# Thresholded attention and a two-layer MLP on one core: the inverses of the softmax sums computed on VectorE alone, a step earlier

## The chip, the cores and the metric

The kernel runs on one core of one Trainium2 chip. The metric is the device time of one execution in microseconds (us); lower is better. The engines go by short names: PE is TensorE (PEld its weight loads), DVE is VectorE, ACT is ScalarE, POOL is GpSimd, SP is SyncE, which issues DMAs. Each engine works through its own queue in order; between engines, semaphores tell when data are ready.

## The reference

q, k and v have 8 batches x 8 heads x 576 rows x 64; the MLP goes from 512 to 2048 and back.

```python
scale = 1.0 / np.sqrt(q.shape[-1])
scores = scale * np.matmul(q, k.transpose(0, 1, 3, 2))
thresh = np.max(scores, axis=-1, keepdims=True) - tau          # tau = 0.02
scores = np.where(scores >= thresh, scores, -1000000000.0)
scores = scores - np.max(scores, axis=-1, keepdims=True)
attn = np.exp(scores)
attn = attn / (np.sum(attn, axis=-1, keepdims=True) + 1e-09)
x = np.matmul(attn, v)                  # heads side by side: 4608 x 512
h = x @ w_in                            # 512 -> 2048
g = np.maximum(0.01 * h, h)
return g @ w_out                        # 2048 -> 512
```

The change concerns one small piece: the row sums of attn, with 1e-9 added, inverted, and brought into the layout in which the product with v is scaled by them.

## The kernel before

**Tiling.** Two heads make a pair, two pairs a couple: 32 pairs, 16 couples. A couple has nine steps (t = 0 to 8); each step computes the scores of 128 rows for two heads, all 576 columns. The main loop runs over c = 0 to 16 and t = 0 to 8; here, block c means the nine steps of couple c. Block 16 has no scores left, only the rest of the work.

**One step.** TensorE computes the scores (`s_mm`, L158) with hi and lo halves in fp16: twelve matmuls into two tiles `s` of two PSUM banks each. VectorE reads each tile, scales it into `sn` and takes the row's extreme into `nmx` (`s_max`, L181), first half (h = 0), then second (h = 1). POOL makes the threshold `nth` out of it (L186). ScalarE takes exp into `e` (L191). One step later VectorE masks (`s_mask`, L214): weights into `W`, and the row sums into one column of `den`, 18 columns for a couple (9 steps x 2 halves). Where `direct` is set, ScalarE does the second half's mask and exp alone (L197 `far`, L201 `W`, with the row sum), and VectorE has one mask less. A transposing DMA on SP's queue brings `W` into `wT` (L220).

**Other work in the steps.** `prep` (steps 6, 7, 8 and 0) turns a new pair's q or k on TensorE into the bank pair `A` (L129); ScalarE makes `hi` of it (L138), and VectorE `lo` (L139). The lo is put off to the end of the step (the list `soon`, behind the masks). `values` (steps 3 and 5) multiplies `wT` with v into `A` (L279); VectorE scales by `rc` into `xT` (L289). The MLP is cut into units, of which each step takes some (`work`): first-layer units (L301, with ScalarE's `gM`, L305) and second-layer units (L316, with ScalarE's `osb`, L327). They share two PSUM banks `u`. A step places half of its units between the two halves of `s_max` and the rest behind. Step 1 takes two or three units from block 3 on; blocks 1 and 2 have none there.

**The sums.** The sums of couple c-1 are complete behind the last mask, `s_mask(c-1, 8)`, which is queued in step 0 of block c. Then, before the change:

- `sums_0`, end of step 0, behind lo: POOL adds 1e-9 (L228, `d1`).
- `sums_1`, step 1, behind VectorE's sn of the first half: VectorE inverts (L234, `rr`), POOL scales by 2048 and rounds to fp16 (L235, `r2[:, 0]`).
- `sums_2`, step 1, behind sn of the second half: VectorE subtracts, which leaves the rounding's remainder in fp16 (L240, `r2[:, 1]`).
- `sums_3`, step 1, ahead of the step's last unit: TensorE turns `r2` with one matmul against the identity (L246) into a bank pair `A`, and ScalarE copies it to `row` (L249).
- `sums_4`, steps 2 and 4: TensorE spreads `row` over the heads with `sel` (L263), ScalarE copies into `rc` (L268), which `values` needs in steps 3 and 5.

There is a single bank pair `A`: prep, sums_3, sums_4 and values follow one another in it, each when its reader is done. The order of the instructions is written out by hand (a manual schedule); each engine keeps it.

Of the kernel before, what the change touches and what calls it, by code (L numbers as in the profile page):

```python
# [11 lines left out]
OP = mybir.AluOpType  # L12
# [4 lines left out]
def kernel(  # L17
# [10 lines left out]
    nc = tc.nc  # L28
# [10 lines left out]
    RS = 1.0 / 2048.0  # L39
# [9 lines left out]
    r2 = sb.tile([128, 2, 64], FP16, name="r2")  # L49
# [61 lines left out]
    soon = []  # L111

    def take(fs):
        r = list(fs)
        fs.clear()
        return r

    def run(fs):
        for f in fs:
            f()  # L120
# [44 lines left out]
    live, dens = {}, {}  # L165

    def s_max(c, t, h, direct):


        s_ = sc[(c, t)][h]  # L170
        if t == 0 and h == 0:
            dens[c] = sb.tile([128, 18], FP32, tag="den", bufs=2, name="den")
        if h == 0:
            sn = sb.tile([128, 2, 576], FP32, tag="sn", bufs=3, name="sn")
            nmx = sb.tile([128, 2], FP32, tag="nmx", bufs=4, name="nmx")
            nth = sb.tile([128, 2], FP32, tag="nth", bufs=4, name="nth")
            e = sb.tile([128, 2, 576], FP16, tag="e", bufs=3, name="e")
            live[(c, t)] = (sn, nmx, nth, e, Ws[wn[0] % len(Ws)], set())
            wn[0] += 1
        sn, nmx, nth, e, w, masked = live[(c, t)]  # L180
        nc.vector.tensor_scalar(  # L181
            out=sn[:, h, :].rearrange("p (a b) -> p a b", a=2), in0=s_[:, :, 0:288],
            scalar1=-BS, scalar2=None, op0=OP.mult, op1=OP.min,
            accum_out=nmx[:, h:h + 1],
        )
        nc.gpsimd.tensor_scalar(  # L186
            out=nth[:, h:h + 1], in0=nmx[:, h:h + 1], scalar1=1.0, scalar2=tau_f,
            op0=OP.mult, op1=OP.add,
        )
        if not direct:  # L190
            nc.scalar.activation(  # L191
                out=e[:, h, :], in_=sn[:, h, :], func=AF.Exp, bias=nmx[:, h:h + 1], scale=-1.0,
            )
        else:
            masked.add(h)
            far = sb.tile([128, 576], FP32, tag="far", bufs=2, name="far")
            nc.scalar.activation(  # L197
                out=far[:, :], in_=sn[:, h, :], func=AF.Prelu, bias=nth[:, h:h + 1], scale=-1.0,
                alpha=BIG,
            )  # L200
            nc.scalar.activation(  # L201
                out=w[:, ds(h * 576, 576)], in_=far[:, :], func=AF.Exp, bias=ntau[:, 0:1], scale=1.0,
                accum_out=dens[c][:, 2 * t + h:2 * t + h + 1],
            )
# [14 lines left out]
        q0 = 512 if t == 8 else t * 128 + (t // 4) * 128  # L219
        nc.sync.dma_start_transpose(out=wTs[c][:, :, ds(q0, 128)], in_=w[:, :])  # L220

    inv, rows, rcs = {}, {}, {}

    def sums_0(c):

        d1 = sb.tile([128, 18], FP32, tag="d1", bufs=1, name="d1")
        rr = sb.tile([128, 18], FP32, tag="rr", bufs=1, name="rr")
        nc.gpsimd.tensor_scalar(out=d1[:, :], in0=dens.pop(c)[:, :], scalar1=1.0, scalar2=1e-9,  # L228
                                op0=OP.mult, op1=OP.add)
        inv[c] = (d1, rr)  # L230

    def sums_1(c):
        d1, rr = inv[c]
        nc.vector.reciprocal(out=rr[:, :], in_=d1[:, :])  # L234
        nc.gpsimd.tensor_scalar(out=r2[:, 0, 0:18], in0=rr[:, :], scalar1=1.0 / RS, scalar2=0.0,  # L235
                                op0=OP.mult, op1=OP.add)

    def sums_2(c):
        d1, rr = inv[c]
        nc.vector.scalar_tensor_tensor(out=r2[:, 1, 0:18], in0=rr[:, :], scalar=1.0 / RS, in1=r2[:, 0, 0:18],  # L240
                                       op0=OP.mult, op1=OP.subtract)

# [132 lines left out]
    def work(n):  # L375
        for _ in range(min(n, len(units))):
            units.pop(0)[1]()

    with tc.manual_schedule():
        nc.scalar.preload_act_table_set("natural_log_exp_and_others")  # L380
        for i, tail in ((0, 0), (1, 0), (0, 1), (1, 1)):
            load_qk(0, i, tail)
        make_identity(nc, I32)
        nc.vector.tensor_copy(out=I16[:, :], in_=I32[:, :])
        nc.vector.memset(ntau[:, :], -tau_f)
        nc.vector.memset(r2[:, :, :], 0.0)
        nc.vector.tensor_tensor(
            out=sel[:, :, :], in0=I32[:, 0:18].unsqueeze(2).to_broadcast([128, 18, 64]),
            in1=I32[:, 64:82].unsqueeze(2).to_broadcast([128, 18, 64]), op=OP.add,
        )  # L390
        nc.vector.tensor_scalar(out=sel[:, :, :], in0=sel[:, :, :], scalar1=RS, scalar2=None, op0=OP.mult)
        for t in Vs:
            nc.vector.memset(t[64:128, :, 0, 4, :], 0.0)
            nc.vector.memset(t[0:64, :, 1, 0, :], 0.0)
        for p in range(1, 3):
            for i in range(2):
                for tail in range(2):
                    load_qk(p, i, tail)
        prep(0, 0)
        prep(0, 1, "s", 2)  # L400
        run(take(soon))
        share = (23, 27, 23, 13, 23, 13, 23, 23, 23)
        credit = 0.0
        w_at = [1 + i for i in range(32)]
        prev = None
        for c in range(NC + 1):
            last = c == NC
            for t in range(NT):
                step = c * NT + t
                if c > 1 and c % 2 == 0 and t == 6:  # L410

                    if c % 4 == 2 and c > 2:
                        push_tail(c // 2 - 3, 1)
                    push_main(c // 2 - 1)
                    if c % 4 == 0:
                        push_tail(c // 2 - 2, 0)
                    if last:
                        push_tail(c // 2 - 2, 1)
                if not last:
                    s_mm(c, t)  # L420


                nxt = {6: (2 * c + 2, 0), 7: (2 * c + 2, 1), 8: (2 * c + 3, 0), 0: (2 * c + 1, 1)}
                if c == 0:
                    nxt[0], nxt[1] = (1, 0), (1, 1)
                pi = nxt.get(t)
                if pi is not None and pi[0] >= NP:
                    pi = None
                if c == 0 and t < 2:
                    prep(*pi)  # L430
                    pi = None

                if c > 0 and t in (3, 5):
                    values(c - 1, t // 2 - 1)

                ahead = [share[i % NT] for i in range(step, (c // 2 * 2 + (0 if c % 2 == 0 and t < 6 else 2)) * NT + 6)]
                credit = min(credit, 1.0) + (len(units) - credit) * share[t] / sum(ahead)
                n = min(int(credit + 0.01), len(units))
                credit -= n
                if not last:  # L440


                    direct = tau_f <= 16.0 and (
                        t not in (3, 7) if c < 3 else t in (3, 5) or not any(u[0] for u in units[:n]))
                    s_max(c, t, 0, False)
                if c > 0 and t == 1:
                    sums_1(c - 1)
                work(n - n // 2)
                if pi is not None:
                    prep(*pi)  # L450
                if c > 0 and t in (2, 4):
                    sums_4(c - 1, t // 2 - 1)
                if not last:
                    s_max(c, t, 1, direct)
                if c > 0 and t == 1:
                    sums_2(c - 1)
                    work(n // 2 - 1)
                    sums_3(c - 1)
                    work(1 if n > 1 else 0)
                else:  # L460
                    work(n // 2)
                if prev is not None:
                    s_mask(*prev)
                    prev = None
                if not last:
                    prev = (c, t)
                run(take(soon))
                if c > 0 and t == 0:
                    sums_0(c - 1)
                if c == 0 and 0 < t < 6:  # L470
                    load_v(0, t - 1)
                if c % 2 == 0 and c > 0 and t >= 4 and c // 2 < B:
                    load_v(c // 2, t - 4)
                for i in range(32):
                    if w_at[i] == step:
                        load_w(i)
                if t < 4 and 2 * c + 3 < NP:
                    load_qk(2 * c + 3, t // 2, t % 2)
                elif 4 <= t < 8 and 2 * c + 4 < NP:
                    load_qk(2 * c + 4, t // 2 - 2, t % 2)  # L480
        work(len(units))
# [35 lines left out]
```

## Time and profile before

| | us |
|---|---|
| median of 3 runs | 540.46 (540.03 to 541.8) |
| span of the profiled execution | 538.3 |
| blocks 5 to 8 (152 to 274 us) | 122.0, PE busy 119.4, ACT 106.8, DVE 105.6, POOL 42.4 |

The span goes from the first to the last instruction of one profiled execution; a run's time also has what lies around it. Three groups of instructions as the page gives them (line, engine, operation, tiles, shape, count; busy us, mean ns; idle before, and what ended it):

```
L181 DVE TENSOR_SCALAR_CACHE_REDUCE sn<-s 128x576 f32<-128x576 f32 x288 | 206.5, 750 | 49.3 <-PE s L158 49.1
L191 ACT ACTIVATE e<-sn,nmx 128x576 f16<-128x576 f32 x196 | 150.5, 769 | 32.4 <-DVE sn L181 32.2
L214 DVE SCALAR_TENSOR_TENSOR W<-sn,nth,e 128x576 f16<-128x576 f32 x196 | 155.6, 814 | 0.0
```

An instruction with an accumulator output is followed by a short row, DVE_READ_ACCUMULATOR, which writes the accumulated column. In a timeline, a row has its start and length in us, the engine, line, operation and tiles, and in brackets how long the engine was idle before it and who ended that. Neighbouring rows of VectorE overlap in the record: the next one starts before the end of the one in front.

### The profile page before, as it was taken

To read this page: it belongs to the slowest core of one execution; us is meant where nothing else is said; L and a number is where in the kernel's file an instruction comes from. 1 tells how busy PE (TensorE), PEld (TensorE's weight loads), DVE (VectorE), ACT (ScalarE), POOL (GpSimd) and SP (SyncE) were. 2 spreads that over 40 slices of the span, in tenths; PEclk is the share of its full clock that TensorE was granted. 3 is DMA by queue.
4 is the path that set the end of the run, shared out by engine and by line. 5 is a ranking of instruction groups with operands and counts; after the bars stand their busy time and mean duration, and the time that the engine had idled before them with its cause. 6 is when DMAs were issued, how large, how long until landed. Compare 5 with 4: busy or idle time off the path is not lost.

```text
span 538.3 us, 12333 instructions
## 1 busy us (share of the span) xinstructions
PE 497.8 (92%) x4384; PEld 272.8 (51%) x4384; DVE 421.7 (78%) x1106; ACT 433.8 (81%) x765; POOL 188.1 (35%) x430
## 2 busy tenths in 40 slices
PE   5678679899999999999999999999999999999996
PEld 3345454454545565454545566455545566445444
DVE  4897989988899878987899878987899878982000
ACT  3887879899878989889888989889888989884622
POOL 0754556443433334222432234323432234331000
PEclk9676969999999999999999999999999999999999
DMA  6999999998998699778999799777998699654001
GB/s 151 150 202 161 175 182 214 200 180 173 172 165 136 139 169 196 140 137 153 183 155 143 132 182 185 142 135 159 183 155 136 132 187 135 111 89 106 39 40 58
DMA packets 266814, 80.50 MB, mean 150 GB/s; under 512 B 251905, under 2 KB 264193, under 8 KB 266753
## 3 DMA queue, kind: packets, MB, share of 16 engines
q1 hardware_dynamic: 249136, 70.68, 72.3%
q0 software_dynamic: 17536, 8.92, 14.2%
q8 instruction: 34, 0.56, 0.4%
q14 instruction: 28, 0.22, 0.1%
q10 hardware_dynamic: 80, 0.13, 0.1%
HBM read 36.70 MB, written 9.44 MB: 86 GB/s over the span
## 4 chain that ended last, share of the span: by engine, by line
PE 43%; ACT 25%; DVE 16%; issue 8%; DMA 4%; POOL 3%; SPq 0%; DVEq 0%; ACTq 0%; POOLq 0%
PE u L316 13%; DVE sn L181 11%; PE u L301 10%; PE s L158 10%; PE A L279 8%; ACT e L191 7%; ACT far L197 5%; ACT W L201 5%; DVE W L214 3%; ACT gM L305 3%; ACT hi L138 3%; POOL nth L186 3%; DMA nat<-in_q_dram 2%; DVE lo L139 1%; ACT rc L268 1%
## 5 line engine op out<-in xcount | busy, mean ns | idle before, releaser
L181 DVE TENSOR_SCALAR_CACHE_REDUCE sn<-s 128x576 f32<-128x576 f32 x288 | 206.5, 750 | 49.3 <-PE s L158 49.1
L186 POOL TENSOR_SCALAR nth<-nmx 128x1 f32<-128x1 f32 x288 | 127.4, 442 | 251.7 <-DVE sn L181 229.5
L191 ACT ACTIVATE e<-sn,nmx 128x576 f16<-128x576 f32 x196 | 150.5, 769 | 32.4 <-DVE sn L181 32.2
L214 DVE SCALAR_TENSOR_TENSOR W<-sn,nth,e 128x576 f16<-128x576 f32 x196 | 155.6, 814 | 0.0
L301 PE MATMUL u<-xT,win 128*128 128x512 f16 x512 | 128.9, 380 | 2.5 <-ACT gM L305 2.5
L316 PE MATMUL u<-wout,gM 128*128 128x512 f16 x512 | 126.2, 380 | 0.0
L158 PEld LDWEIGHTS <-hi 64*128 64x128 f16 (+1 forms) x1280 | 65.1, 99 | 70.2 <-issue 54.9
L158 PE MATMUL s<-hi,hi 64*128 64x288 f16 x512 | 86.2, 300 | 10.3 <-DVE sn L181 8.8
L158 PE MATMUL s<-lo,hi 64*128 64x288 f16 (+1 forms) x640 | 92.2, 294 | 0.0
L158 PE MATMUL s<-hi,lo 64*128 64x288 f16 (+1 forms) x640 | 92.1, 294 | 0.0
L301 PEld LDWEIGHTS <-win 128*128 128x128 f16 x768 | 58.7, 98 | 56.5 <-issue 20.1
L305 ACT ACTIVATE gM<-u 128x512 f16<-128x512 f32 x128 | 74.6, 588 | 11.7 <-PE u L301 11.7
L197 ACT ACTIVATE far<-sn,nth 128x576 f32<-128x576 f32 x92 | 71.0, 771 | 13.8 <-POOL nth L186 11.6
L201 ACT ACTIVATE W<-far,ntau 128x576 f16<-128x576 f32 x92 | 71.3, 775 | 3.0
L316 PEld LDWEIGHTS <-gM 128*128 128x128 f16 x512 | 44.7, 98 | 51.3 <-issue 12.3
L139 DVE SCALAR_TENSOR_TENSOR lo<-A,hi 128x512 f16<-128x512 f32 (+1 forms) x63 | 47.6, 756 | 14.2 <-ACT hi L138 13.7
L129 PE MATMUL A<-I,nat 128*128 128x128 f32 x283 | 44.6, 288 | 9.9 <-DVE lo L139 4.7
L279 PE MATMUL A<-wT,V 128*64 128x288 f16 x640 | 47.5, 297 | 1.5 <-ACT rc L268 1.1
L129 PEld LDWEIGHTS A<-I,nat 128*128 128x128 f32 x283 | 35.2, 147 | 25.2 <-DVE lo L139 10.0
L138 ACT ACTIVATE hi<-A 128x512 f16<-128x512 f32 (+1 forms) x63 | 40.0, 636 | 7.6 <-PE A L129 7.6
L279 PEld LDWEIGHTS <-V 128*64 128x64 f16 x640 | 36.6, 113 | 11.9 <-issue 8.4
L158 PEld LDWEIGHTS <-lo 64*128 64x128 f16 (+1 forms) x640 | 32.1, 99 | 12.6 <-issue 8.9
(44 smaller groups left out, 292.1 us busy)
## 6 DMA issues: line engine op xcount, KB each, us to landing
nat<-in_q_dram SPq DMA_DIRECT2D x32, 256.0 KB, 3.8
nat<-in_k_dram SPq DMA_DIRECT2D x32, 256.0 KB, 3.9
out_dram<-osb SPq DMA_DIRECT2D x16, 512.0 KB, 3.0
wT<-W SPq DMA_TRANSPOSE x144, 3.9
V<-in_v_dram POOLq DMA_DIRECT2D x8, 256.0 KB, 6.1
win<-in_moe_w_in_dram POOLq DMA_DIRECT2D x16, 128.0 KB, 5.2
V<-in_v_dram POOLq DMA_DIRECT2D x16, 128.0 KB, 4.7
wout<-in_moe_w_out_dram POOLq DMA_DIRECT2D x16, 128.0 KB, 4.3
```

What stands on the lines that cost most here:

```text
L129: nc.tensor.matmul(out=pt[0:128, ds(c * 128, 128)], lhsT=t[0:128, 4 * i + c, :, :].rearrange("p h d -> p (h d)"), rhs=I32[:, :], is_transp ...
L158: nc.tensor.matmul(out=out[h][po, half, 0:288], lhsT=qk[p][i][a][r, cols], rhs=qk[p][1][b][r, ds(half * 288, 288)], start=(ti == 0), stop= ...
L181: nc.vector.tensor_scalar(out=sn[:, h, :].rearrange("p (a b) -> p a b", a=2), in0=s_[:, :, 0:288], scalar1=-BS, scalar2=None, op0=OP.mult, ...
L186: nc.gpsimd.tensor_scalar(out=nth[:, h:h + 1], in0=nmx[:, h:h + 1], scalar1=1.0, scalar2=tau_f, op0=OP.mult, op1=OP.add,)
L191: nc.scalar.activation(out=e[:, h, :], in_=sn[:, h, :], func=AF.Exp, bias=nmx[:, h:h + 1], scale=-1.0,)
L197: nc.scalar.activation(out=far[:, :], in_=sn[:, h, :], func=AF.Prelu, bias=nth[:, h:h + 1], scale=-1.0, alpha=BIG,)
L201: nc.scalar.activation(out=w[:, ds(h * 576, 576)], in_=far[:, :], func=AF.Exp, bias=ntau[:, 0:1], scale=1.0, accum_out=dens[c][:, 2 * t + ...
L214: nc.vector.scalar_tensor_tensor(out=w[:, ds(h * 576, 576)], in0=sn[:, h, :], scalar=nth[:, h:h + 1], in1=e[:, h, :], op0=OP.is_le, op1=OP ...
L279: nc.tensor.matmul(out=t[ds(h * 64, 64), half, 0:288], lhsT=vb[:, g, h, kb, :], rhs=wT[:, 4 * h + kb, ds(e * 576 + half * 288, 288)], star ...
L301: nc.tensor.matmul(out=t[:, ts(j, N)], lhsT=w_in16[:, gi, ts(j0 + j, 128)], rhs=xs[gi], start=(gi == 0), stop=(gi == NG - 1), skip_group_c ...
L305: nc.scalar.activation(out=g_out, in_=t[:, 0:nj * N].rearrange("p (j n) -> p j n", j=nj), func=AF.Prelu, bias=0.0, scale=1.0, alpha=0.01)
L316: nc.tensor.matmul(out=t[:, :], lhsT=g_in(j), rhs=w_out16[:, j, :], start=(j == 0), stop=(j == NJ - 1), skip_group_check=True,)
```

## The change

Add, reciprocal, multiply and subtract all go to VectorE and stand in one function, `sums_0`, which is queued in step 0 directly behind the last mask (and its transposing DMA), ahead of the put-off `lo`. POOL has no part in it any more; `sums_1` and `sums_2` are gone. `sums_3` (the turn on TensorE and ScalarE's copy) stays in step 1 and moves up: it stands behind the first half of the step's units and ahead of sn of the second half. The rest of the units then follow in one piece.

```diff
     def sums_0(c):
         d1 = sb.tile([128, 18], FP32, tag="d1", bufs=1, name="d1")
         rr = sb.tile([128, 18], FP32, tag="rr", bufs=1, name="rr")
-        nc.gpsimd.tensor_scalar(out=d1[:, :], in0=dens.pop(c)[:, :], scalar1=1.0, scalar2=1e-9,
-                                op0=OP.mult, op1=OP.add)
-        inv[c] = (d1, rr)
-
-    def sums_1(c):
-        d1, rr = inv[c]
+        nc.vector.tensor_scalar(out=d1[:, :], in0=dens.pop(c)[:, :], scalar1=1e-9, scalar2=None, op0=OP.add)
         nc.vector.reciprocal(out=rr[:, :], in_=d1[:, :])
-        nc.gpsimd.tensor_scalar(out=r2[:, 0, 0:18], in0=rr[:, :], scalar1=1.0 / RS, scalar2=0.0,
-                                op0=OP.mult, op1=OP.add)
-
-    def sums_2(c):
-        d1, rr = inv[c]
+        nc.vector.tensor_scalar(out=r2[:, 0, 0:18], in0=rr[:, :], scalar1=1.0 / RS, scalar2=None, op0=OP.mult)
         nc.vector.scalar_tensor_tensor(out=r2[:, 1, 0:18], in0=rr[:, :], scalar=1.0 / RS, in1=r2[:, 0, 0:18],
                                        op0=OP.mult, op1=OP.subtract)
...
                     s_max(c, t, 0, False)
+                work(n - n // 2)
                 if c > 0 and t == 1:
-                    sums_1(c - 1)
-                work(n - n // 2)
+                    sums_3(c - 1)
                 if pi is not None:
                     prep(*pi)
...
                 if not last:
                     s_max(c, t, 1, direct)
-                if c > 0 and t == 1:
-                    sums_2(c - 1)
-                    work(n // 2 - 1)
-                    sums_3(c - 1)
-                    work(1 if n > 1 else 0)
-                else:
-                    work(n // 2)
+                work(n // 2)
                 if prev is not None:
                     s_mask(*prev)
                     prev = None
                 if not last:
                     prev = (c, t)
-                run(take(soon))
                 if c > 0 and t == 0:
                     sums_0(c - 1)
+                run(take(soon))
```

More of the change, by code (lines that the diff above doesn't have):

```diff
@@ L220, in s_mask @@
         nc.sync.dma_start_transpose(out=wTs[c][:, :, ds(q0, 128)], in_=w[:, :])
-    inv, rows, rcs = {}, {}, {}
+    rows, rcs = {}, {}
     def sums_0(c):
```

## The prediction

> **What bounds the kernel now.** I read the page's busy shares, then the list of waits, then the timeline around the steps that the change touches.
>
> ```profile
> PE 497.8 (92%) x4384; PEld 272.8 (51%) x4384; DVE 421.7 (78%) x1106; ACT 433.8 (81%) x765; POOL 188.1 (35%) x430
> ```
>
> No engine fills the span, so each stage has to be read by itself. The steps are chained: the scores of a step (TensorE, L158) wait until VectorE has read both halves of the step before (L181), and L181 waits for the scores. A delay of one is a delay of all that follows.
>
> ```profile
> PEld L246 <- DVE r L240: 17.4, 16, 2.6
> PE A L246 <- DVE r L240: 9.1, 12, 2.1
> ```
>
> The list of waits (us in total, times, longest): the little turn of the inverted sums (L246) holds TensorE's in-order queue. The matmul's own idle time is 9.1 us, and that is all the change can take from TensorE; the weight load's 17.4 lies mostly under running matmuls. By the timelines at blocks 1 to 15 (block c is the nine steps of couple c; the turned sums are those of couple c-1) the idle times are 2.11, 1.55, 1.33, 0.86, 0.34, 0.10, 0.40, 0.61, 0.34, 0.10, 0.40, 0.44, 0.34, 0.10, 0.40; 0.07 in block 16.
>
> ```profile
> 277.35 0.09 DVE L214 DVE_READ_ACCUMULATOR W<-sn,nth,e 128x1 f32 x1
> 277.35 0.82 DVE L139 SCALAR_TENSOR_TENSOR lo<-A,hi 128x640 f16<-128x640 f32 x1
> ...
> 278.09 0.75 DVE L181 TENSOR_SCALAR_CACHE_REDUCE sn<-s 128x576 f32<-128x576 f32 x1
> ...
> 278.76 0.27 DVE L234 RECIPROCAL rr<-d 128x18 f32<-128x18 f32 x1
> ...
> 278.94 0.70 DVE L181 TENSOR_SCALAR_CACHE_REDUCE sn<-s 128x576 f32<-128x576 f32 x1
> 278.94 0.78 ACT L191 ACTIVATE e<-sn,nmx 128x576 f16<-128x576 f32 x1 [0.57 <-DVE sn L181]
> ...
> 279.56 0.18 DVE L240 SCALAR_TENSOR_TENSOR r<-rr,r 128x18 f16<-128x18 f32 x1
> 279.62 1.06 ACT L305 ACTIVATE gM<-u 128x512 f16<-128x512 f32 x2
> 279.64 0.82 DVE L214 SCALAR_TENSOR_TENSOR W<-sn,nth,e 128x576 f16<-128x576 f32 x1
> ...
> 279.79 0.23 PE L246 MATMUL A<-I,r 128*128 128x128 f16 x1 [0.34 <-DVE r L240]
> ...
> 280.25 1.02 PE L301 MATMUL u<-xT,win 128*128 128x512 f16 x4 [0.23 <-ACT gM L305]
> ...
> 281.21 0.30 PE L158 MATMUL s<-hi,hi 64*128 64x288 f16 x2
> ```
>
> Block 9, steps 0 and 1 (start, length, idle before). VectorE goes without a pause from the mask to lo, to sn of step 1: here VectorE sets the time. ScalarE's exp (L191) idles 0.57 us for that sn; behind it stand the gM copies; the unit behind L246 waits for the first gM (0.23), since there are two u banks; the scores of step 2 follow at 281.21. So the chain from VectorE's step 0 to the scores of step 2 has no slack, and it does not go through L246.
>
> ```profile
> 306.97 0.08 DVE L214 DVE_READ_ACCUMULATOR W<-sn,nth,e 128x1 f32 x1
> ...
> 307.55 0.82 DVE L139 SCALAR_TENSOR_TENSOR lo<-A,hi 128x640 f16<-128x640 f32 x1 [0.50 <-ACT hi L138]
> ...
> 309.99 0.23 PE L246 MATMUL A<-I,r 128*128 128x128 f16 x1
> 310.06 1.03 PE L316 MATMUL u<-wout,gM 128*128 128x512 f16 x4
> ...
> 311.02 0.30 PE L158 MATMUL s<-hi,hi 64*128 64x288 f16 x2
> ```
>
> Block 10, where the units are of the second layer (L316). One mask on VectorE is missing (ScalarE masked that half), lo waits for hi, 0.58 us after it could have started, and TensorE is the late one: nothing of ScalarE stands between L246 and the scores.
>
> **What the change adds to VectorE in step 0.** Add, reciprocal, multiply and subtract now stand between the last mask and lo (L139), each reading what the one in front wrote. The trace has one such pair:
>
> ```profile
> 1.57 1.30 DVE L387 TENSOR_TENSOR sel<-I 128x1152 f16<-128x1152 f32 x1
> 2.90 0.46 DVE L391 TENSOR_SCALAR sel<-sel 128x1152 f16<-128x1152 f16 x1
> ```
>
> The second starts 0.03 us after the end of the first; independent neighbours overlap (mask to read-accumulator 0.74 for a length of 0.82). Lengths: reciprocal 0.262, subtract (L240) 0.175, both rows of before. A VectorE tensor_scalar on 128x18 does not stand in the trace: below it lies the 128x64 memset (0.11), above it the 128x128 cast (0.23); I take 0.175, the row of its own size. Behind the subtract an independent instruction starts after 0.08 (279.56 to 279.64). So from the read-accumulator to lo: 0.08 + 4 x 0.03 + 0.175 + 0.26 + 0.175 + 0.08 = **0.90 us** (call it S). Low end, if dependent ones overlapped as others do: 3 x 0.08 + 0.18 (278.76 to 278.94) = 0.43. High end, with 0.09 per handover (read-accumulator's end to ScalarE's start, 278.85 to 278.94) and 0.23 per tensor_scalar: 1.24.
>
> [...]
>
> **What it removes.** From VectorE's step 1 the reciprocal (0.17) and subtract (0.08); they stand behind sn of the first half, so they help the second sn and not the exp that ScalarE waits for. From POOL two instructions of 0.22 us, which nobody but this chain waited for (the far copy's wait for nth, 0.23 in block 10, may shorten; it ends in slack). L246 itself moves up, between the unit(s) of the first half and sn of the second: its inputs are ready a step earlier, its bank A is free when lo ends (block 9: 278.17 + 0.90 = 279.1, TensorE gets there at 279.45). The row copy (0.26 us) moves ahead of the second exp on ScalarE; that exp is read by a mask a step later and the next gM keeps its place: 0. No DMA moves; the last mask's transpose is issued in front of the sums, as before.
>
> **Block by block**, at the scores of step 2:
> - Blocks 5, 7, 9, 11, 13, 15 (units of the first layer): the whole S goes through sn, exp, gM and the unit to the scores; taking away L246's wait gives nothing, for the unit behind it waits for gM. 6 x 0.90 = **+5.4**.
> - Blocks 1, 2 (no units): lo already waits 0.10, so sn moves by 0.80. L158 needs the second sn, 0.82 after its start (37.16 to 37.98); the second sn now starts 0.68 after the first: 39.42 + 0.80 + 0.68 + 0.82 = 41.72 against 41.34. With a matmul pair already gone, +0.33 each: **+0.7**.
> - Block 3: lo waits 0.84 for hi, so sn moves 0.06; L246's idle time of 1.33 goes, the scores start at 98.5 in place of 99.68, but VectorE's two masks hold the next sn: 99.86 in place of 100.62. **-0.8**.
> - Block 4: 125.97 + 0.78 + 1.50 = 128.25 against 128.70: **-0.4**.
> - Blocks 8, 12: the wait for hi (0.91) covers S; L246's idle time goes: **-0.6 and -0.4**.
> - Blocks 6, 10, 14: 0.58 of S is covered, sn moves 0.32, scores could start at 310.1, TensorE is there at 310.9: **-0.1** each.
> - Block 16: TensorE is full of units: 0.
>
> Sum: 5.4 + 0.7 - 0.8 - 0.4 - 1.0 - 0.3 = **+3.6 us**, 538.3 to 541.9 in the profiled execution. The median of the runs (540.46) lies 2.2 above the span; so 544.1. With S = 0.43: 6 x 0.43 - 2 x 0.1 - 0.9 (block 4) - 2.1 = -0.6, 539.9. With S = 1.24: 7.4 + 1.4 - 0.1 - 2.1 = +6.6, 547.1.
>
> **Rivals.**
> - The four overlap or their handover costs nothing (S = 0.43): 539.9. For it: VectorE overlaps all its neighbours. Against: L391 starts only behind L387's end. [...]
> - **Faster:** the place is L246; TensorE at 92% is the limit, and VectorE's delay in step 0 vanishes in its idle time in front of step 2's sn (0.94 in block 9, 1.29 in block 10). Then the idle times of L246 go but for blocks 1 and 2 (3.7, which turn into the wait for sn): 9.5 - 3.7 = 5.8 less, 534.7. It decides if the unit behind L246 isn't held by gM; the 0.23 and 0.17 there in the six blocks speak against it, the ten other blocks for it.
> - Slower still: the row copy in front of the second exp is not free; ScalarE (81%) hands 0.26 on in each of 15 blocks, +3.9 on top: 548.0. Against: ScalarE idles again at the first exp of step 2 (1.01 in block 9).
>
> **Numbers.** Forecast 0.60, overlap 0.13, faster 0.17, slower still 0.10. A difference under 0.3% (1.6 us) can't be told from none: faster is below 538.8, slower above 542.1. Faster: 0.15 of its rival and 0.03 of overlap, 0.18. Same: 0.10 of overlap, 0.02, and 0.05 of the forecast's low end, 0.17. Slower: 0.65. The range goes from 539.0 (overlap, less the 0.9 that runs of one kernel differ) to 547.2 (the high S); outside lie the faster rival and a little of the slowest. The forecast alone: 541.9 to 546.5.
>
> **What would show it.** Right: sn of step 1 in blocks 5 to 15 (odd) starts about 0.9 us later after the last mask, four small VectorE rows without overlap, L246 without a wait for VectorE, L301 behind it waiting longer for gM, step 1 to 2 in the even blocks shorter by 0.1 to 0.6. Wrong: from the mask to lo less than 0.5 us (where the sum turns to a gain), or the odd blocks keeping their length, because gM comes in time.

## The result, and the profile after

| | before | after |
|---|---|---|
| median of the runs, us | 540.25 (539.88 to 541.8, 4 runs) | 545.04 (544.71 to 545.35, 4 runs) |
| span of the profiled execution, us | 538.3 | 543.5 |

The changed kernel is slower: ratio 1.0078, 95% interval 1.0062 to 1.0094. The forecast was 544.1.

The busy shares of the page of the changed kernel, and four rows of its list of waits (engine, line waited for: us in total, times, longest). Lines have moved: the turn is now L237 (L246 before), first-layer units L292 (L301), gM L296 (L305), second-layer units L307 (L316), row L240 (L249), the spreading of row L254 (L263); the sums are L228 to L231.

```profile
PE 500.9 (92%) x4384; PEld 275.5 (51%) x4384; DVE 429.9 (79%) x1138; ACT 433.1 (80%) x765; POOL 180.1 (33%) x398
```

```profile
ACT e L191 <- DVE sn L181: 41.2, 52, 2.8
...
PE u L292 <- ACT gM L296: 11.4, 10, 1.7
...
PE A L237 <- DVE lo L139: 2.7, 3, 1.6
PEld L237 <- DVE r L231: 2.2, 3, 1.2
```

The shares say nothing; the waits do. TensorE's wait at the turn fell from 9.1 to 2.7 us, and what is left there, in blocks 1, 2 and 4, waits for lo (in three blocks the turn's weight load still waits for the sums as well, 2.2 us together). But the units' wait for gM, 2.5 us before, is now 11.4, and ScalarE's exp waits 41.2 us for sn in place of 32.2. The wait did not go, it moved one link on.

Block 9 of the changed kernel in the timeline (start, length in us, engine, line, operation, tiles; in brackets the idle time before and who ended it):

```profile
278.69 0.08 DVE L214 DVE_READ_ACCUMULATOR W<-sn,nth,e 128x1 f32 x1
278.81 0.18 DVE L228 TENSOR_SCALAR d<-den 128x18 f32<-128x18 f32 x1
279.02 0.27 DVE L229 RECIPROCAL rr<-d 128x18 f32<-128x18 f32 x1
...
279.32 0.18 DVE L230 TENSOR_SCALAR r<-rr 128x18 f16<-128x18 f32 x1
279.54 0.18 DVE L231 SCALAR_TENSOR_TENSOR r<-rr,r 128x18 f16<-128x18 f32 x1
279.63 0.82 DVE L139 SCALAR_TENSOR_TENSOR lo<-A,hi 128x640 f16<-128x640 f32 x1
...
280.37 0.75 DVE L181 TENSOR_SCALAR_CACHE_REDUCE sn<-s 128x576 f32<-128x576 f32 x1
...
280.63 0.22 PE L237 MATMUL A<-I,r 128*128 128x128 f16 x1
...
281.22 0.78 ACT L191 ACTIVATE e<-sn,nmx 128x576 f16<-128x576 f32 x1 [1.50 <-DVE sn L181]
...
281.90 1.06 ACT L296 ACTIVATE gM<-u 128x512 f16<-128x512 f32 x2
...
282.52 1.69 PE L292 MATMUL u<-xT,win 128*128 128x512 f16 x4 [1.68 <-ACT gM L296]
...
284.14 0.42 PE L158 MATMUL s<-hi,hi 64*128 64x288 f16 x2
```

The four rows of the sums do not overlap: each starts 0.03 to 0.04 us behind the end of the one it reads. From the read-accumulator to lo it is 0.94 us, where lo followed at once before. The turn no longer waits for the sums here. Then the chain of the forecast: sn, exp (idle 1.50 in place of 0.57), gM, the unit (1.68 in place of 0.23), the scores of step 2. From the unit at 282.52 on, this block also has a slow TensorE clock (0.51 granted from 282.70 to 286.10), which the last section takes up; the waits in front of it are not touched by that (the unit's wait is 1.68 to 1.69 in all six odd blocks from 5 on).

Block 10, where the units are of the second layer, TensorE's matmuls alone, in the changed kernel:

```profile
311.85 1.90 PE L307 MATMUL u<-wout,gM 128*128 128x512 f16 x8
313.58 0.22 PE L237 MATMUL A<-I,r 128*128 128x128 f16 x1
313.64 1.03 PE L307 MATMUL u<-wout,gM 128*128 128x512 f16 x4
...
314.60 0.30 PE L158 MATMUL s<-hi,hi 64*128 64x288 f16 x2
```

The same two units and the turn before the change:

```profile
307.99 1.90 PE L316 MATMUL u<-wout,gM 128*128 128x512 f16 x8
309.99 0.23 PE L246 MATMUL A<-I,r 128*128 128x128 f16 x1
```

From the two units to the scores it is 2.75 us; before it was 3.03 (307.99 to 311.02). TensorE goes through without a pause, and 0.28 are gained.

Laid side by side by the start of each block's first sn, the two traces differ so (us, plus is longer after):

| block | 0 | 1 | 2 | 3 | 4 | 5 | 6 | 7 | 8 | 9 | 10 | 11 | 12 | 13 | 14 | 15 |
|---|---|---|---|---|---|---|---|---|---|---|---|---|---|---|---|---|
| forecast | 0 | +0.33 | +0.33 | -0.8 | -0.4 | +0.9 | -0.1 | +0.9 | -0.6 | +0.9 | -0.1 | +0.9 | -0.4 | +0.9 | -0.1 | +0.9 |
| measured | +0.46 | +1.01 | +0.35 | -0.82 | -0.37 | +0.94 | -0.27 | +0.95 | -0.78 | +2.52 | -0.27 | +0.94 | -0.61 | +0.94 | -0.27 | +0.94 |

Block 15 is taken up to its last sn.

### The profile page after: what moved, and what is told of

It is laid out like the page before. It is cut to its first block, busy times and chain, and to the rows that moved or that the text cites. A ratio compares the mean times of both kernels' runs of the same rounds, so it can differ in the third digit from the quotient of the medians.

```text
span 543.5 us, 12343 instructions
## 1 busy us (share of the span) xinstructions
PE 500.9 (92%) x4384; PEld 275.5 (51%) x4384; DVE 429.9 (79%) x1138; ACT 433.1 (80%) x765; POOL 180.1 (33%) x398
## 4 chain that ended last, share of the span: by engine, by line
PE 54%; ACT 18%; DVE 14%; issue 7%; DMA 4%; POOL 2%; SPq 0%; DVEq 0%; ACTq 0%; POOLq 0%
PE u L307 19%; PE s L158 13%; PE u L292 11%; DVE sn L181 9%; PE A L270 8%; ACT e L191 5%; DVE W L214 4%; ACT far L197 3%; ACT W L201 3%; ACT gM L296 2%; PE A L129 2%; DMA nat<-in_q_dram 2%; POOL nth L186 2%; ACT hi L138 1%; DMA wT<-W 1%
## 5 line engine op out<-in xcount | busy, mean ns | idle before, releaser
L191 ACT ACTIVATE e<-sn,nmx 128x576 f16<-128x576 f32 x196 | 150.5, 769 | 41.4 <-DVE sn L181 41.2
L292 PE MATMUL u<-xT,win 128*128 128x512 f16 x512 | 129.7, 382 | 11.5 <-ACT gM L296 11.4
L307 PE MATMUL u<-wout,gM 128*128 128x512 f16 x512 | 125.6, 380 | 0.0
L158 PEld LDWEIGHTS <-hi 64*128 64x128 f16 (+1 forms) x1280 | 67.2, 100 | 74.1 <-issue 58.2
L158 PE MATMUL s<-hi,hi 64*128 64x288 f16 x512 | 89.5, 302 | 12.1 <-DVE sn L181 10.5
L158 PE MATMUL s<-hi,lo 64*128 64x288 f16 (+1 forms) x640 | 95.0, 299 | 0.0
L158 PE MATMUL s<-lo,hi 64*128 64x288 f16 (+1 forms) x640 | 95.0, 298 | 0.0
L292 PEld LDWEIGHTS <-win 128*128 128x128 f16 x768 | 58.9, 98 | 66.9 <-issue 30.0
L296 ACT ACTIVATE gM<-u 128x512 f16<-128x512 f32 x128 | 74.7, 588 | 12.0 <-PE u L292 12.0
L307 PEld LDWEIGHTS <-gM 128*128 128x128 f16 x512 | 44.7, 98 | 52.4 <-issue 12.8
```

The lines of the kernel that those rows point to most:

```text
L158: nc.tensor.matmul(out=out[h][po, half, 0:288], lhsT=qk[p][i][a][r, cols], rhs=qk[p][1][b][r, ds(half * 288, 288)], start=(ti == 0), stop= ...
L191: nc.scalar.activation(out=e[:, h, :], in_=sn[:, h, :], func=AF.Exp, bias=nmx[:, h:h + 1], scale=-1.0,)
L292: nc.tensor.matmul(out=t[:, ts(j, N)], lhsT=w_in16[:, gi, ts(j0 + j, 128)], rhs=xs[gi], start=(gi == 0), stop=(gi == NG - 1), skip_group_c ...
L296: nc.scalar.activation(out=g_out, in_=t[:, 0:nj * N].rearrange("p (j n) -> p j n", j=nj), func=AF.Prelu, bias=0.0, scale=1.0, alpha=0.01)
L307: nc.tensor.matmul(out=t[:, :], lhsT=g_in(j), rhs=w_out16[:, j, :], start=(j == 0), stop=(j == NJ - 1), skip_group_check=True,)
```

## The experiments

Theory: VectorE's chain of four, 0.94 us ahead of sn of step 1, goes through exp, gM and the unit behind the turn to the next scores in the odd blocks; in the even ones it lies under lo's wait for hi and under TensorE, and there the sums' readiness is a gain. Rivals: what costs is the delay of lo (and of bank A), or the new place of the turn and of the row copy. The table has the change of a block's length against the kernel before, for all of them, read in the same way as above.

| kernel | median us | ratio to before, 95% interval | blocks 5, 13 | 7, 11, 15 | 6, 10, 14 | 8 | 12 |
|---|---|---|---|---|---|---|---|
| after | 545.04 | 1.0078 [1.0062, 1.0094] | +0.94 | +0.94 | -0.27 | -0.78 | -0.61 |
| e1 sums behind lo | 545.38 | 1.0089 [1.0061, 1.0116] | +0.81 | +0.81 | -0.27 | -0.61 | -0.45 |
| e2 turn in its old place | 546.33 | 1.0115 [1.0100, 1.0130] | +0.94 | +0.94 | +0.12 | -0.39 | -0.22 |
| e3 before, turn in step 2 | 538.31 | 0.9964 [0.9951, 0.9977] | +0.03 | +0.06 | -0.10 | -0.78 | -0.10 |
| e4 after, units ahead of exp | 535.19 | 0.9911 [0.9893, 0.9929] | -0.36 | -0.35 | -0.28 | -0.78 | -0.61 |
| e5 two more in the chain | 549.19 | 1.0171 [1.0138, 1.0205] | +1.36 | +1.36 | -0.27 | -0.78 | -0.61 |
| e6 before, units ahead of exp | 538.60 | 0.9975 [0.9958, 0.9993] | -0.39 | -0.33 | +0.23 | +0.01 | +0.01 |
| e7 split, early, units ahead | 530.72 | 0.9816 [0.9789, 0.9844] | -0.90 | -0.90 | -0.27 | -0.78 | -0.62 |
| e8 split, early | 537.10 | 0.9940 [0.9918, 0.9962] | +0.12 | +0.12 | -0.27 | -0.78 | -0.62 |

Where two or three blocks stand in one column, it is their mean; they differ by no more than 0.12.

**e1: is it lo, or sn?** The sums change places with lo.

```diff
-                if c > 0 and t == 0:
-                    sums_0(c - 1)
                 run(take(soon))
+                if c > 0 and t == 0:
+                    sums_0(c - 1)
```

> The four instructions of the sums change places with lo: lo first, then the sums, both still ahead of sn of step 1. Theory (what costs is VectorE's time ahead of sn of step 1): the odd blocks 5 to 15 stay 0.94 us longer than before the change each; the even blocks lose the cover of lo's wait for hi, blocks 3, 8 and 12 lose up to 0.9, 0.2 and 0.2; about 546 us, 1 more than the changed kernel. Rival (what costs is that lo, and with it bank A, comes later): the odd blocks go back to their old length, about 540.

lo is as early as before the change, and the odd blocks are still 0.81 longer. The rival of the late lo falls. Sn comes 0.81 and not 0.94 later, in every block: mask and lo stand again as before the change, where the read-accumulator and lo start together (277.35 in block 9), so that its 0.08 and the 0.04 from its end to the first of the four (278.69 to 278.81 in the changed kernel) no longer count; that these 0.12 account for the difference of 0.13 is an estimate from these rows. Blocks 3, 8 and 12 lost their cover, as expected (block 3: -0.18 in place of -0.82). The median is not 1 us above the changed kernel but 0.3. The odd blocks gave 0.13 each back, which I had not counted; but the five runs fall into two groups, 542.2 and 542.3 (the second is the profiled one) and 545.4 to 545.8, and what parts the groups is not shown, so the blocks and not the median carry this experiment.

**e2: is it the place of the turn?** Sums as in the changed kernel, the turn back ahead of the last unit.

```diff
-                if c > 0 and t == 1:
-                    sums_3(c - 1)
...
-                work(n // 2)
+                if c > 0 and t == 1:
+                    work(n // 2 - 1)
+                    sums_3(c - 1)
+                    work(1 if n > 1 else 0)
+                else:
+                    work(n // 2)
```

> The sums as in the changed kernel, the turn (matmul and row copy) back in its old place, ahead of the last unit of step 1. Theory (the turn's wait goes because the sums are ready a step earlier, its place does nothing): 545 us within 0.7, the odd blocks +0.94 each against the kernel before, the even ones unchanged against the changed kernel. Rival (the row copy ahead of the second exp, or the turn's matmul ahead of the unit, carries part of the loss): 541 to 543, the odd blocks shorter by some tenths each.

The odd blocks do not move, so the turn's place has no part in the loss. But "its place does nothing" was wrong: the even blocks from 6 on are 0.39 longer than in the changed kernel, block 4 is 0.94 longer, and the median of 546.3 lies above the 545.7 that was allowed for. Block 10 of e2, timeline:

```profile
315.55 0.78 ACT L201 ACTIVATE W<-far,ntau 128x576 f16<-128x576 f32 x1
...
316.32 0.25 ACT L240 ACTIVATE row<-A 128x128 f16<-128x128 f32 x1
...
316.63 0.41 PE L254 MATMUL A<-row,sel 128*128 128x128 f16 x5 [0.23 <-ACT row L240]
```

With the scores of step 2 early, the row copy, queued behind ScalarE's far and W, is the next to be late, and TensorE waits for it (in the changed kernel, no such wait stands in front of L254 in any block). The earlier place is needed to keep the gain of the even blocks.

**e3: is the wait at the turn worth its idle time?** The kernel before, with the turn alone put off.

```diff
                 if not last:
                     s_mm(c, t)
+                if c > 0 and t == 2:
+                    sums_3(c - 1)
...
-                    work(n // 2 - 1)
-                    sums_3(c - 1)
-                    work(1 if n > 1 else 0)
-                else:
-                    work(n // 2)
+                work(n // 2)
```

> The kernel before the change, with the sums as they were on VectorE and POOL, and the turn alone put off: behind the scores of step 2. Theory (the wait at the turn costs only where the unit behind it isn't held by gM anyway): blocks 1 and 2 -0.25 each, 3 -0.8, 4 -0.9, 8 -0.6, 12 -0.4, the others 0 to -0.1; about 536.8 us, 3.5 less than before. Rival (the wait costs wherever it shows, in the odd blocks too): -0.3 to -0.4 more in each of six odd blocks, about 534.5. If the turn only waits in its new place instead: 540.

Block 9 of e3, the unit that stood behind the turn:

```profile
278.61 1.02 PE L301 MATMUL u<-xT,win 128*128 128x512 f16 x4 [0.80 <-ACT gM L305]
```

The odd blocks gain nothing, though the turn with its 0.34 to 0.40 of waiting no longer stands in step 1: the unit waits 0.80 for gM in place of 0.23. That is the theory against its rival. At sn of step 2 the other blocks were 0.33 to 1.09 earlier, but all except blocks 3 and 8 gave most of it back between steps 2 and 3. In blocks 1, 2, 4 and 12 the trace shows why: the row now comes too late, and TensorE's spreading of it waits 0.92, 0.92, 0.77 and 0.36 us. In blocks 6, 10 and 14, which gave back 0.23, the record has no wait there, and the cause is not shown. So the gain is half of what was expected (538.31 against 536.8).

**e4: does the delay go by exp and gM?** The changed kernel, with the order of ScalarE's queue changed.

```diff
+                    if c > 0 and t == 1:
+                        work(n - n // 2)
                     s_max(c, t, 0, False)
-                work(n - n // 2)
+                if last or not (c > 0 and t == 1):
+                    work(n - n // 2)
```

> The changed kernel, with the first half of step 1's units queued ahead of sn and exp of the first half, so that ScalarE copies their gM ahead of that exp. Theory (in the odd blocks VectorE's delay reaches the scores of step 2 through exp, gM and the unit behind the turn): that unit no longer waits, scores of step 2 come when the second sn is done, and the next sn behind VectorE's two masks: about 1.2 less in each of six odd blocks, 538 us. Rival (the delay goes straight from sn to the scores, ScalarE's order does nothing): 545.

Block 9 of e4, timeline:

```profile
275.06 1.02 PE L292 MATMUL u<-xT,win 128*128 128x512 f16 x4 [0.32 <-ACT gM L296]
...
275.66 0.75 DVE L181 TENSOR_SCALAR_CACHE_REDUCE sn<-s 128x576 f32<-128x576 f32 x1
...
275.92 0.22 PE L237 MATMUL A<-I,r 128*128 128x128 f16 x1
275.98 1.03 PE L292 MATMUL u<-xT,win 128*128 128x512 f16 x4
...
276.93 0.49 PE L158 MATMUL s<-hi,hi 64*128 64x288 f16 x2
...
278.49 0.09 DVE L214 DVE_READ_ACCUMULATOR W<-sn,nth,e 128x1 f32 x1
278.49 0.76 DVE L181 TENSOR_SCALAR_CACHE_REDUCE sn<-s 128x576 f32<-128x576 f32 x1
```

The sums still hold up sn by 0.94 us, but the unit follows the turn at once, and sn of step 2 follows VectorE's second mask at once. The odd blocks are 1.3 us shorter than in the changed kernel, the even ones the same: the delay did go by ScalarE's queue. The whole came out at 535.2, not 538. Laid beside the changed kernel's, the profiled execution (533.9) has 0.6 from the 1.3 in place of 1.2 in each odd block, 1.6 from block 9, which had no slow clock here (last section), and 1.8 from blocks 0 to 2, in which the two kernels have the same order.

**e5: does the chain's length count?** Two more multiplications by 1 in it.

```diff
-        nc.vector.reciprocal(out=rr[:, :], in_=d1[:, :])
...
+        nc.vector.tensor_scalar(out=d2[:, :], in0=d1[:, :], scalar1=1.0, scalar2=None, op0=OP.mult)
+        nc.vector.tensor_scalar(out=d3[:, :], in0=d2[:, :], scalar1=1.0, scalar2=None, op0=OP.mult)
+        nc.vector.reciprocal(out=rr[:, :], in_=d3[:, :])
```

> The changed kernel with two more multiplications by 1 in the chain of the sums, each reading the one before (0.21 us each from start to start). Theory (the chain's length goes through in the odd blocks, and in the even ones is covered by lo's wait for hi and by TensorE being late): each odd block from 5 to 15 +0.42, block 3 and the even ones 0 to +0.4 at sn of step 1 and 0 to +0.1 at step 2; about 548 us, 2.5 to 3 more than the changed kernel. Rival (VectorE has slack in step 0 and the loss is elsewhere): 545.

Against the changed kernel it is +0.42 in each odd block (0.47 in block 9, which had a stretch of slow clock in both), and 0.00 in the even ones from 6 on, as expected. In the odd blocks VectorE's time is the kernel's time one for one; in these even ones another 0.42 us cost nothing. Blocks 3 and 4 miss the expectation: at sn of step 2 they are 0.42 later, where at most 0.1 was expected, so they had no cover left. These two are 0.8 us of the 1.2 by which the median exceeds 548; the rest is not accounted for.

**e6: what of e4 is the order alone?** The order of e4 in the kernel before.

> The kernel before the change, with the first half of step 1's units ahead of sn and exp, as in e4. Theory (with gM early, the unit behind the turn is held by the turn's wait for VectorE alone): the odd blocks gain about 0.3 each at sn of step 2, the even ones nothing; about 538 us. Rival (the units' order is the whole gain of e4, and the sums a step earlier bring nothing with it): 535, as e4.

Block 9 of e6, TensorE's matmuls alone:

```profile
278.99 0.23 PE L246 MATMUL A<-I,r 128*128 128x128 f16 x1 [0.34 <-DVE r L240]
279.05 1.03 PE L301 MATMUL u<-xT,win 128*128 128x512 f16 x4
```

As the theory had it: -0.32 to -0.39 in the odd blocks, and no gain in the even ones (6, 10 and 14 lose 0.23). The turn's wait for VectorE is still there (0.34 here, 0.40 in blocks 7, 11 and 15); what has gone is the wait of the unit behind it for gM, which was 0.23 and 0.17 in the same blocks before. The order alone is worth 1.9 us (540.55 in the same series to 538.6) and not the 4.9 of e4 (540.06 to 535.19). The blocks say where the difference lies: in the odd blocks e4 gains no more than e6 (-0.36 in both), so there the early sums add nothing as a chain of four; what e4 has beyond e6 are blocks 3, 4 and the even ones, which the changed kernel had gained already.

**e8 and e7: the gain without the chain.** The sums a step earlier as in the change, but with POOL's two instructions as before. sums_0 is POOL's add alone, behind the last mask; sums_1 (reciprocal on VectorE, multiplication on POOL) stands behind lo, so that POOL adds while lo runs; sums_2 (the subtract) stands behind the first sn. The main lines of e8 against the changed kernel (the heads of the three functions are left out); e7 has the order of e4 besides.

```diff
-        nc.vector.tensor_scalar(out=d1[:, :], in0=dens.pop(c)[:, :], scalar1=1e-9, scalar2=None, op0=OP.add)
+        nc.gpsimd.tensor_scalar(out=d1[:, :], in0=dens.pop(c)[:, :], scalar1=1.0, scalar2=1e-9,
+                                op0=OP.mult, op1=OP.add)
...
-        nc.vector.tensor_scalar(out=r2[:, 0, 0:18], in0=rr[:, :], scalar1=1.0 / RS, scalar2=None, op0=OP.mult)
+        nc.gpsimd.tensor_scalar(out=r2[:, 0, 0:18], in0=rr[:, :], scalar1=1.0 / RS, scalar2=0.0,
+                                op0=OP.mult, op1=OP.add)
...
                 run(take(soon))
+                if c > 0 and t == 0:
+                    sums_1(c - 1)
...
                     s_max(c, t, 0, False)
+                if c > 0 and t == 1:
+                    sums_2(c - 1)
```

> As e7, without the units ahead. Theory: the odd blocks 0.17 longer than before the change in place of 0.94, the even blocks keep the gain of the changed kernel; about 538.5 us, 1.5 to 2 less than before. Rival (what the odd blocks lost hangs on the place of the sums and the turn, not on the chain's length): about 545, as the changed kernel.

> The sums go a step earlier as in the change, but POOL adds and multiplies as before: add behind the last mask, reciprocal behind lo in step 0, multiply on POOL, subtract behind the first sn of step 1, the turn where the change has it; the units ahead as in e4. Theory (the loss is the chain of four on VectorE, the gain is that the sums are ready at the turn): sn of step 1 comes 0.17 later than before the change in place of 0.94, so 0.7 less than e4 in each of six odd blocks and some in 1 and 2: about 531 us. Rival (POOL's handovers make the turn or VectorE wait again): 535 or more.

Block 9 of e7, VectorE's timeline (the reciprocal is L236 there, the subtract L242):

```profile
273.01 0.82 DVE L139 SCALAR_TENSOR_TENSOR lo<-A,hi 128x640 f16<-128x640 f32 x1
273.75 0.26 DVE L236 RECIPROCAL rr<-d 128x18 f32<-128x18 f32 x1
273.92 0.70 DVE L181 TENSOR_SCALAR_CACHE_REDUCE sn<-s 128x576 f32<-128x576 f32 x1
...
274.54 0.17 DVE L242 SCALAR_TENSOR_TENSOR r<-rr,r 128x18 f16<-128x18 f32 x1
274.63 0.75 DVE L181 TENSOR_SCALAR_CACHE_REDUCE sn<-s 128x576 f32<-128x576 f32 x1
```

The reciprocal and the subtract lie between independent neighbours and cost 0.17 and 0.09 from start to start. With e8 the odd blocks are 0.12 longer than before the change in place of 0.94, and the even ones from 6 on keep all they had gained: 537.1, 0.6% faster than before. That separates the two halves of the change: the earlier readiness and the earlier turn are a gain of some 3 us (540.55 in the same series to 537.10), the chain of four is the loss. With the units ahead as well (e7), 530.7, which is **1.8% faster than the kernel before** and the best here.

## Why the prediction came out as it did

- **The chain on VectorE** (S): 0.90 forecast, 0.94 measured. The tensor_scalar on 128x18, which the trace of before did not have, takes 0.177 (the add) and 0.180 (the multiplication), as the row of its own size said (0.175). The rival of the overlapping four is out: each starts 0.03 to 0.04 behind the end of the one it reads.
- **Odd blocks**: +0.90 each forecast, +0.94 measured (block 9 aside), by the way that was named; e4 and e5 show it from two sides, and e8, which takes the chain apart, is left with 0.12.
- **Even blocks and 3, 4**: the sign right everywhere, the size in 3 and 4 to 0.05. In 6, 8, 10, 12 and 14 the gain was 0.17 to 0.21 larger than forecast. The term that was too small is TensorE's idle time at the turn, which the prediction took for all that TensorE could gain. It was read from the matmul's own row (0.10, 0.61, 0.44), but the recorded end of a matmul is not the earliest start of the next: now the turn starts 0.17 us ahead of the recorded end of the units before it (313.58 against 311.85 + 1.90), so that much of the wait had lain under the record of running matmuls. Row plus 0.17 gives 0.27, 0.78 and 0.61, which is what the blocks gained.
- **Blocks 1 and 2**: +0.7 forecast, +1.36 measured. At sn of step 2 they are 0.23 and 0.24 later, about two thirds of the forecast 0.33 each; most of the rest comes up behind step 3, where the edit changes nothing. e4, which has the same order as the changed kernel in these blocks, is the same 0.23 and 0.24 later at step 2 and ends at -0.25 for the two. So the rest is no part of the change's path as far as these runs show: in the first 80 us the clock goes up and down (the page's slices 2 to 6 are at 6 to 9 tenths in both), block 0, which no edit touches, came out 0.46 longer here, and the other kernels show -0.9 to +2.0 for blocks 1 and 2.
- **The faster rival** (VectorE's delay vanishes in its idle time) holds in the even blocks from 6 on, not in the odd ones, where gM decided, as its condition said. **Slower still** (the row copy ahead of the exp) is out: e2 moves it back and is slower.
- **The sum**: +3.6 forecast, +5.3 in the profiled execution, +4.8 in the median. Blocks 3 to 15 give +2.2 where 2.9 were forecast, once block 9's 1.6 above its neighbours are set aside. Those 1.6 and the 1.8 of blocks 0 to 2 make up the rest, less 0.4 ahead of the first sn and behind the last. So the path and the two sizes that decide were right, but that the total came out within 1 us of the forecast is in part luck, errors of both signs that partly cancel: the even blocks from 6 on took off 0.9 more than was said, while the slow clock of block 9 (1.6) and blocks 0 to 2 (1.2 more than forecast) put on what nobody had forecast.

## What to carry to other kernels

Before a short chain of dependent instructions is moved to one engine "where it is ready", follow what stands directly behind it in that engine's queue to the next matmul: at some 0.2 us apiece four tiny instructions cost 0.94 us in a stage that this engine bounds, and nothing where it waits anyway. Between independent neighbours the subtract cost 0.09 and the reciprocal 0.17, so spreading them over two engines and between other work beat gathering them. And where a copy that frees a bank is queued behind work that is needed only a step later, putting the copy first can be worth more than the change under study (here 6.4 us, e8 to e7).

## What was not expected of the hardware

In block 9 of the changed kernel a stretch of slow clock followed the longer stall, and the block is 2.52 us longer than before where the other odd blocks from 5 on are 0.94 to 0.95. Two stretches of 3.4 us, in the windows view (length, then busy us of each engine, granted TensorE clock, DMA share, GB/s):

```profile
279.30:282.70 3.40, 1.40 (x7) 0.58 (x6) 3.34 (x10) 1.90 (x4) 0.89 (x2) 1.00 0.96 198
282.70:286.10 3.40, 3.40 (x17) 1.16 (x16) 0.88 (x3) 1.69 (x4) 0.00 (x0) 0.51 0.51 96
```

TensorE was busy for 41% of one stretch, and the granted clock was 0.51 in the next, where the four matmuls at 282.52 took 1.69 us in place of 1.02. e5 shows the same in its block 9, behind a stretch that was 43% busy by its matmul rows; behind the first 90 us of the two kernels, the next emptiest stretches of the same grid (in the traces of before and after, the clock changes only at distances of a multiple of 3.41 us), 46% (from 156.45 in the changed kernel) and 47%, were followed by full clock. The share of the matmul rows does not decide it alone, though: early in the changed kernel, stretches that were 53% and 57% busy (from 33.57 and from 57.46 us) were followed by a granted clock of 0.50. What brings the clock down is not shown by these runs. The grid does not lie alike in the two traces (carried back, its first line lies 1.04 us behind the first instruction in the one of before and 2.85 in the one of after), so that a stall of the same length could fall into one stretch or be parted between two; that this is what spreads the runs of one kernel was not tried. On record, the granted clock over the whole span speaks against it as the only cause: in e1 it was 0.968 in the two short runs, and 0.964, 0.974 and 0.974 in the three long ones.
